# Loading the first input tile as one transfer instead of two halves on two queues

## The chip, the cores and the metric

The kernel runs on one core of a Trainium2 chip. Its time is the device time of one execution in microseconds (us), given as the median of several runs. A profile is one further execution, recorded by the hardware; its span runs from the first to the last instruction. The engines are TensorE (PE; its weight loads are listed apart as PEld), VectorE (DVE), ScalarE (ACT), GpSimd (POOL) and SyncE (SP). In this kernel SP and ACT issue DMAs, each into a queue of its own (q1 in the profile is SP's, q10 is ACT's), and both queues are served by the same 16 DMA engines.

## The reference

One mixer block and one MLP on an input of 2048 rows and 512 columns, in bfloat16:

```
h  = gelu(layernorm(x) @ w1)              # 512 x 512
hs = the four column quarters of h, shifted along the rows by +1, -1, +2, -2 (zeros come in)
x1 = x + hs @ w2                          # 512 x 512
out = x1 + gelu(layernorm(x1) @ w3) @ w4  # 512 x 1792, 1792 x 512
```

## The kernel before

The 2048 rows are 16 tiles of 128 rows; tile t holds, on partition p, row 16 p + t, so that each partition's row of a tile is 1 KB of contiguous memory. All weights and all of x stay in on-chip memory.

Each tile goes through the same steps. `stats` (L314, VectorE) and `aggr` (L317) give mean and variance. The inverse root comes, for tiles 0 to 3, from a square root on ScalarE (`rstd_act`, L325) and a reciprocal on VectorE (`rcp`, L331), and for later tiles from GpSimd (`rstd_pool`, L338 and L347). `norm` (L367 on VectorE) writes the normalized tile, which is transposed either by TensorE (`peT`, L389), with a copy out by ScalarE or VectorE (`evacT`, L401, L403), for tiles 0 to 9, or by a transposing DMA on SP (`dmaT`, L377) for the others. Then `mm1` (L440, and L456 for the first pair) multiplies two tiles at a time with w1, `gelu1` applies the activation, `mm2` (L515) multiplies with w2 and `add1` (L527) adds x. The second normalization, `mm3` (L542), `gelu2` (L555), `mm4` (L568) and the last addition (L582) follow, and `add2` stores each output tile (L586). The last output tile is done in two parts: 384 columns stored from SP's queue and then 128 columns stored from ACT's queue.

The order on each engine is written out by hand: a list of calls appends operations to one sequence per engine, and the `emit` function puts a semaphore wait ahead of an operation for each result that it needs and that its engine does not already know of. Every DMA has a semaphore of its own.

On VectorE the sequence starts: stats of tiles 0 and 1, their aggregates, stats of tile 2, reciprocal and norms of tiles 0 and 1, stats of tile 3, aggregates of 2 and 3, the copy of tile 1's transpose, reciprocal and norms of 2 and 3, stats of tiles 4 and 5, aggregates, stats of 6 and 7, norms of 4 and 5. TensorE begins with 12 multiplications of constants (`keep_warm`, L600), then the transposes of tiles 0 and 1, the first half of `mm1` of that pair, the transposes of tiles 2 and 3, the second half, three quarters of `mm1` of the second pair, and the transposes of tiles 4 and 5.

SP's queue issues all loads, one behind the other and without a wait: half of tile 0, tiles 1, 2 and 3 singly, w1 in two parts, tiles 4 and 5, 6 and 7, 8 to 11, 12 to 15, w2, w3. ACT's queue holds two DMAs in the whole kernel: the other half of tile 0 as ACT's first instruction, ahead of the load of the square root table (L590), and the last store.

Of the kernel before, what the change touches and what calls it, by code (L numbers as in the profile page):

```python
# [5 lines left out]
P = 128  # L6
# [151 lines left out]
def bass_standalone__mixer_s_mlp__prompt_kernel(  # L158
# [22 lines left out]
    x3 = x[0].rearrange("(p t) d -> p t d", t=NT)  # L181
# [3 lines left out]
    with ExitStack() as es:  # L185
        sb = lambda name, shape, dt: es.enter_context(nc.sbuf_tensor(name, shape, dt))
        x_sb = sb("x_sb", [P, NT, D], BF16)
# [25 lines left out]
        pr = Prog()  # L213
# [4 lines left out]
        g_x = [Gen() for _ in range(NT)]  # L218
# [18 lines left out]
        def load_x(eng, t0, n):  # L237
            pr.op(eng, f"x{t0}",
                  lambda e: e.dma_start(x_sb[:, t0 : t0 + n, :], x3[:, t0 : t0 + n, :]),
                  w=g_x[t0 : t0 + n], dma=True)  # L240

        def load_x_rows(eng, t, p0, n):
            pr.op(eng, f"x{t}_{p0}",
                  lambda e: e.dma_start(x_sb[p0 : p0 + n, t, :], x3[p0 : p0 + n, t, :]),
                  w=[g_x[t]], dma=True)

        def load_w(name, dst, src, c0=0, n=DC):

# [354 lines left out]
            pr.op("pe", "warm", f, w=[g])  # L603


        load_x_rows("sp", 0, 0, P // 2)
        load_x_rows("act", 0, P // 2, P // 2)
        for t in range(1, 4):
            load_x("sp", t, 1)
        load_w("w1", w1_sb, w1, 0, 2)  # L610
        load_w("w1", w1_sb, w1, 2, 2)
# [199 lines left out]
```

## Time and profile before

| what | value |
|---|---|
| time, median of 3 runs | 140.81 us (140.53 to 141.4) |
| profiled execution | 140.27 us |
| its span | 138.0 us |
| granted TensorE clock | 1.000 |
| issue of SP's half of tile 0 | 0.72 us, 2.4 us to landing |
| issue of ACT's half of tile 0 | 0.73 us, 3.0 us to landing |
| issue of tile 1 | 1.36 us, 2.7 us to landing |
| issue of tiles 4 and 5 | 3.90 us, 4.9 us to landing |
| first stats instruction (L314) | starts at 3.85 us |

The profile is read in views. The busy totals say how long each engine worked; the chain that ended last follows the work back from the last instruction, at each step to what released it; the timeline lists instructions in order of time; the list of waits adds up what each engine waited for. Times in views count from the start of the span. A DMA lands in 16 parts, one for each DMA engine, and the trace records when each part signalled; the DMA has landed when the last has.

### The profile page before, as it was taken

What the parts mean: (1) busy time and instruction counts of PE and PEld (TensorE: products, weight loads), DVE (VectorE), ACT (ScalarE), POOL (GpSimd) and SP (SyncE); (2) the same over time, 40 slices, a digit from 0 to 9 for tenths busy, and PEclk for the clock granted to TensorE, in tenths of its full rate; (3) what the DMA queues carried; (4) which work ended last, traced back from release to release, by engine and by line L of the source; (5) the groups of instructions that cost most, each with busy time, mean ns of one, the idle gap of its engine ahead of it and who ended that gap; (6) DMA issues with size and microseconds to landing.
All of it is one profiled execution on the core that took longest, in us unless ns stands there. A gap on an engine that the chain in (4) does not pass through costs nothing.

```text
span 138.0 us, 1802 instructions
## 1 busy us (share of the span) xinstructions
PE 131.6 (95%) x694; PEld 66.9 (48%) x706; DVE 50.2 (36%) x116; ACT 56.3 (41%) x71; POOL 16.9 (12%) x58
## 2 busy tenths in 40 slices
PE   7678999999999999999999999999999999999993
PEld 3265876665444444444444444444444444444452
DVE  0899999998958400000223000022300002232222
ACT  4097862496596796554000455400045540000000
POOL 2005342463333300000000000000000000000000
DMA  2899935434445499200111100011110001111111
GB/s 81 270 320 306 405 104 114 78 72 85 70 85 112 104 231 295 95 5 0 38 38 38 38 0 5 0 38 38 38 38 0 5 0 38 38 38 38 38 68 46
DMA packets 19047, 11.90 MB, mean 86 GB/s; under 512 B 12640, under 2 KB 18016, under 8 KB 19040
## 3 DMA queue, kind: packets, MB, share of 16 engines
q1 hardware_dynamic: 18816, 11.70, 30.7%
q10 hardware_dynamic: 224, 0.10, 0.3%
q8 instruction: 5, 0.08, 0.3%
q14 instruction: 2, 0.02, 0.0%
HBM read 6.82 MB, written 2.10 MB: 65 GB/s over the span
## 4 chain that ended last, share of the span: by engine, by line
PE 84%; DVE 10%; DMA 2%; ACT 1%; issue 1%; DVEq 0%
PE ps L568 35%; PE ps L542 35%; PE ps L515 8%; DVE st L314 6%; PE ps L440 5%; DMA x_sb<-in_x_dram 2%; DVE xn L367 1%; DVE x_sb L527 1%; DVE mv L317 1%; PE ps L389 1%; ACT xT L401 1%; ACT sdv L325 0%; DVE o_sb L582 0%; DVE rstd L331 0%; DVEq L134 0%
## 5 line engine op out<-in xcount | busy, mean ns | idle before, releaser
L542 PE MATMUL ps<-x1T,w_sb 128*128 128x512 bf16 x219 | 48.9, 379 | 0.3
L568 PE MATMUL ps<-w_sb,h2T 128*128 128x512 bf16 (+2 forms) x234 | 48.7, 366 | 0.2
L555 ACT ACTIVATE h2T<-ps 128x1024 bf16<-128x1024 f32 x28 | 28.3, 1020 | 39.0 <-PE ps L542 38.9
L582 DVE TENSOR_TENSOR o_sb<-ps,x_sb 128x512 bf16<-128x512 f32 (+2 forms) x17 | 11.2, 660 | 78.5 <-PE ps L568 78.5
L568 PEld LDWEIGHTS ps<-w_sb,h2T 128*128 128x128 bf16 x238 | 22.8, 98 | 25.9
L542 PEld LDWEIGHTS ps<-x1T,w_sb 128*128 128x128 bf16 x224 | 21.9, 98 | 26.4
L314 DVE BATCH_NORM_STATS2 st<-x_sb 128x6 f32<-128x512 bf16 x32 | 20.4, 675 | 3.9 <-DMA x_sb<-in_x_dram 3.9
L515 PE MATMUL ps<-w_sb,hT 128*128 128x512 bf16 x61 | 14.8, 379 | 0.2
L440 PE MATMUL ps<-xT,w_sb 128*128 128x256 bf16 x112 | 13.9, 273 | 0.5 <-ACT xT L401 0.4
L362 ACT ACTIVATE xn<-x_sb,nmr,rstd 128x512 bf16<-128x512 bf16 x16 | 12.0, 808 | 4.5 <-POOL nmr L352 4.5
L440 PEld LDWEIGHTS ps<-xT,w_sb 128*128 128x128 bf16 x112 | 10.7, 98 | 3.3 <-ACT xT L401 1.1
L527 DVE TENSOR_TENSOR x_sb<-ps,x_sb 128x512 bf16<-128x512 f32 x16 | 10.7, 683 | 3.1 <-PE ps L515 3.1
L347 POOL TENSOR_TENSOR rstd<-vpe,neghalf 128x2 f32<-128x2 f32 x14 | 9.9, 707 | 0.5
L515 PEld LDWEIGHTS ps<-w_sb,hT 128*128 128x128 bf16 x64 | 6.3, 98 | 6.3
L501 ACT ACTIVATE hT<-ps 128x1024 bf16<-128x1024 f32 x6 | 6.2, 1026 | 4.3 <-PE ps L440 4.3
L338 POOL TENSOR_SCALAR vpe<-mv 128x2 f32<-128x2 f32 x14 | 3.1, 220 | 28.4 <-DVE mv L317 28.3
L401 ACT ACTIVATE xT<-ps 128x512 bf16<-128x512 bf16 x9 | 4.9, 593 | 3.3 <-PE ps L389 3.3
L367 DVE TENSOR_SCALAR xn<-x_sb,mv,rstd 128x512 bf16<-128x512 bf16 x16 | 5.9, 410 | 0.3
L600 PE MATMUL ps<-const-bfloat16-1.0 128*128 128x512 bf16 x12 | 4.4, 542 | 0.8 <-PEq L796 0.8
L389 PE MATMUL ps<-ident,xn 128*128 128x128 bf16 x40 | 3.3, 220 | 1.4 <-DVE xn L367 1.3
L317 DVE BATCH_NORM_AGGREGATE mv<-st 128x2 f32<-128x6 f32 x32 | 4.5, 170 | 0.0
L389 PEld LDWEIGHTS ps<-ident,xn 128*128 128x128 bf16 x40 | 2.5, 98 | 2.5 <-DVE xn L367 2.2
(21 smaller groups left out, 16.5 us busy)
## 6 DMA issues: line engine op xcount, KB each, us to landing
w_sb<-in_w_dram SPq DMA_DIRECT2D x4, 512.0 KB, 4.7
out_dram<-o_sb SPq DMA_DIRECT2D x15, 128.0 KB, 1.8
w_sb<-in_w_dram SPq DMA_DIRECT2D x1, 1792.0 KB, 13.2
x_sb<-in_x_dram SPq DMA_DIRECT2D x2, 512.0 KB, 7.0
w_sb<-in_w_dram SPq DMA_DIRECT2D x3, 256.0 KB, 4.7
x_sb<-in_x_dram SPq DMA_DIRECT2D x2, 256.0 KB, 5.2
x_sb<-in_x_dram SPq DMA_DIRECT2D x3, 128.0 KB, 2.7
x1T<-xn SPq DMA_TRANSPOSE x16, 2.5
```

Of the source, the lines that this page charges most:

```text
L314: pr.op("dve", f"st{q}", lambda e: e.bn_stats(st6[:, q, :], a), r=[g], w=[g_st[q]])
L347: lambda e: e.tensor_tensor(rstd[:, q : q + 2], vpe[:, q : q + 2], neghalf[:], ALU.pow),
L362: lambda e: e.activation(xn[:, s, :], a, ACT_F.Identity, bias=nmr[:, q : q + 1], scale=rstd[:, q : q + 1]),
L367: lambda e: e.tensor_scalar(xn[:, s, :], a, mv[:, q, 0:1], rstd[:, q : q + 1], ALU.subtract, ALU.mult),
L389: ins = e.transpose(dst[:, P * c : P * (c + 1)], xn[:, q % NXN, P * c : P * (c + 1)], ident[:])
L440: ins = e.matmul(dst, w1_sb[:, dc, P * fc : P * (fc + 1)], xT[:, dc, 256 * p : 256 * (p + 1)], start=(dc == 0), stop=(dc == DC - 1))
L515: ins = e.matmul(bankap(b), hT[:, j, c : c + P], w2_sb[:, j, :], start=(j == 0), stop=(j == DC - 1))
L527: lambda e: e.tensor_tensor(x1_sb[:, t, :], bankap(b), x_sb[:, t, :], ALU.add),
L542: ins = e.matmul(bankap(b + i), w3_sb[:, dc, P * fc : P * (fc + 1)], x1T[:, dc, 512 * s : 512 * (s + 1)], start=(dc == 0), stop=(dc == DC ...
L555: pr.op("act", f"g2_{s}_{fp}", lambda e: e.activation(o, a, ACT_F.Gelu_apprx_tanh), r=gens, w=[g])
L568: ins = e.matmul(ps[:, 512 * b : 512 * b + n], h2T[:, fc, s % 2, P * i : P * (i + 1)], w4_sb[:, fc, c0 : c0 + n], start=(fc == 0), stop=(f ...
L582: lambda e: e.tensor_tensor(o_sb[:, s, 0:n], ps[:, 512 * b : 512 * b + n], x1_sb[:, t, c0 : c0 + n], ALU.add),
```

## The change

Tile 0 is loaded by one DMA of 128 rows on SP's queue, by the same helper and in the same loop as tiles 1 to 3. The DMA that ACT issued is gone, and with it the helper for loading some rows of a tile. All else is as it was; the lines below the helper have numbers that are 5 lower, and those below the loop 7 lower.

```diff
-        def load_x_rows(eng, t, p0, n):
-            pr.op(eng, f"x{t}_{p0}",
-                  lambda e: e.dma_start(x_sb[p0 : p0 + n, t, :], x3[p0 : p0 + n, t, :]),
-                  w=[g_x[t]], dma=True)
-
...
-        load_x_rows("sp", 0, 0, P // 2)
-        load_x_rows("act", 0, P // 2, P // 2)
-        for t in range(1, 4):
+        for t in range(4):
             load_x("sp", t, 1)
```

## The prediction

> **What bounds the kernel now.** I read the busy totals first, then the chain that ended last in order of time, then the timelines of VectorE and of the two queues. The totals:
>
> ```profile
> span 138.0 us, 1802 instructions
> PE 131.6 (95%) x694; PEld 66.9 (48%) x706; DVE 50.2 (36%) x116; ACT 56.3 (41%) x71; POOL 16.9 (12%) x58
> ```
>
> TensorE is busy for 95% of the span, so a change to one input load can only matter where TensorE isn't yet, or no longer, the bound. The chain (start, length, what) says where:
>
> ```profile
> 0.73 3.02 DMA x_sb<-in_x_dram
> ...
> 3.85 1.29 DVE st L314 x2
> ...
> 8.15 0.74 DVE xn L367 x2
> 8.89 1.25 DVE st L314 x2
> ...
> 11.56 0.42 DVE xn L367
> 11.98 0.05 issue
> 12.03 0.41 PE ps L389 x4
> ...
> 135.71 0.02 issue
> 135.73 0.29 DVE o_sb L582
> ```
>
> Up to 12.03 us the chain is the load of x tile 0 and then VectorE nearly without a gap; from 13.60 on it is TensorE back to back up to 135.71; then the last eviction, its store from ACT's queue and the end. A time saved or lost at 12.03 passes through to the end, because TensorE has no idle stretch later in which to absorb it (idle time after 12.03 is 1.05 us in total, in pieces). The change touches two places of this chain: its first row, and, through ACT's queue, its end.
>
> **The load of tile 0.** Issues of the two queues (start, length):
>
> ```profile
> 0.72 0.57 SPq L244 DMA_DIRECT2D x_sb<-in_x_dram  x1
> 0.73 0.57 ACTq L244 DMA_DIRECT2D x_sb<-in_x_dram  x1
> 1.36 0.56 SPq L239 DMA_DIRECT2D x_sb<-in_x_dram  x1
> ```
>
> From issue to landing these take 2.4, 3.0 and 2.7 us. The landing records put the last part of SP's half at 3.10, of ACT's half at 3.75 and of tile 1 at 4.08; st0 starts at 3.85, 0.10 after ACT's half. So ACT's half is the late one: its packets begin at 2.39 against 2.12 for SP's, and on four of the 16 engines its last rows come at 3.14 and later, after packets of tile 1.
>
> The changed kernel issues 128 rows at 0.72 on SP. The issue doesn't grow with the rows (0.57 for 64, 0.56 for the 128 of tile 1), so SP's later issues stay where they are; no instruction of theirs is moved past another. The trace has no 128-row load that comes first on an idle queue, so I bound its landing: from below SP's half, 2.38 us (3.10), since twice the rows can't land sooner; from above tile 3, issued at 2.43 and landed 3.9 us later into a backlog (0.72 + 3.9 = 4.64). The nearest row is tile 1, same shape and next in line: 2.72, so 3.45. I expect 3.3 to 3.45, 0.3 to 0.45 us before now.
>
> The Trainium skill (DMA: Bandwidth & Descriptors, section "Rules for kernel authors") says of two transfers to disjoint partition halves that they share the same engines either way, and advises one transfer of 128 partitions. The trace shows the shared engines (packets of both queues between 2.39 and 2.84), but also that the second half lands 0.65 us after the first. By the rule alone the front would change by 0 and the time stay at 140.8; by the rows tile 0 gains 0.3 to 0.45, and what becomes of that is the next step.
>
> **Who is late next.** Tile 1, then tile 3, then tiles 4 and 5. st1 needs tile 1 (4.08, and 0.1 for the wait: 4.18 against 4.46 now), st3 needs tile 3 (last part at 6.35, against its start at 6.68). So st3 can come forward by at most 0.33, and everything up to the second pair of norms by some 0.25 to 0.3. Then comes st4, which reads tiles 4 and 5:
>
> ```profile
> 6.36 0.41 DVE L367 TENSOR_SCALAR xn<-x_sb,mv,rstd 128x512 bf16<-128x512 bf16 x1
> 6.68 0.69 DVE L314 BATCH_NORM_STATS2 st<-x_sb 128x6 f32<-128x512 bf16 x1
> ```
>
> ```profile
> 8.48 0.41 DVE L367 TENSOR_SCALAR xn<-x_sb,mv,rstd 128x512 bf16<-128x512 bf16 x1
> 8.85 0.69 DVE L314 BATCH_NORM_STATS2 st<-x_sb 128x6 f32<-128x512 bf16 x1
> ```
>
> Where nothing is waited for, a stats instruction begins before the record of the norm ahead of it ends: 6.36 + 0.41 = 6.77 against 6.68, an overlap of 0.09. At st4 the overlap is 8.89 − 8.85 = 0.04: it started 0.045 us late. Tiles 4 and 5, issued at 3.90, land 4.9 us later; the last of their 16 parts is recorded at 8.82, the other 15 by 8.38. So st4 already waited for that load, too briefly for the list of waits to show. Whatever VectorE gains before it is turned into a wait there, unless the load comes earlier too.
>
> Does it? From 3.2 us on the DMA engines carry a backlog (busy share 0.88 in 3.2 to 4, 0.89, 0.71, 1.00, 0.81, 0.98 in the next stretches), so tiles 4 and 5 land when the slowest engine has moved its share of all bytes before them, and these bytes are the same: 512 KB of tiles 0 to 3, 512 KB of w1, 256 KB of tiles 4 and 5. Only one small completion packet of 9 ns per engine goes. In the front I therefore count **0.0**; bounds −0.36 (0.31 through tile 3's landing plus the 0.045) and, if the slowest part of tiles 4 and 5 shifts the other way by its lead over the rest (8.82 − 8.38), +0.44.
>
> **What goes from ACT.** Its DMA issue at 0.73 (0.57 us) goes, and with it the table load moves from 1.33 to about 0.73. Hidden: ACT then waits 2.6 us for VectorE's aggregates before its first sqrt, so nothing follows. One of two semaphore waits ahead of st0 (0.02) goes too, into the same wait at st4.
>
> **The end.** The last store, 32 KB, leaves by ACT's queue:
>
> ```profile
> 0.73 0.57 ACTq L244 DMA_DIRECT2D x_sb<-in_x_dram  x1
> ...
> 136.05 0.36 ACTq L586 DMA_DIRECT2D out_dram<-o_sb  x1
> ```
>
> It lands at 137.53, last of all (SP's last one at 137.2), so it is on the path. It is ACT's second DMA now and becomes its first. The trace prices a first DMA of this queue only at the start: 0.57 for the issue, against 0.36 for the second, and 1.66 us from issue to first packet, against 0.86. SP's first two take 0.57 and 0.56, later stores 0.33 to 0.36. Bounds: 0, if the start alone was slow (SP's second was as slow as its first, which speaks for that), and 0.86 → 1.66, **+0.8**, if all of it belongs to a queue's first use (part of that is a load's way through memory, so it is an outer bound). I take the difference of ACT's own two issues, **+0.2**.
>
> **Sum.** 0.0 + 0.2 = +0.2 us. The profiled execution took 140.27 (span 138.0 and 2.27 around it), so 140.5 by its own time. It lies 0.54 under the median of 140.81 and below the lowest of the three runs (140.53), so on the scale of the median: **141.0**. One per cent, 1.4 us, is about what a measurement of this kernel can tell from no change; this sum is far inside.
>
> **Rivals.**
> *The lead survives (faster).* Tiles 4 and 5 land earlier by 0.3, since one slow engine sets them and it may get its first rows sooner; then norms, transposes and TensorE all come forward by 0.25 to 0.3, and the end costs nothing: 140.81 − 0.3 = 140.5. For it: ACT's half is plainly the late piece of the first wait. Against it: 15 of 16 parts are there by 8.38 in any case, and the bytes ahead of the sixteenth are unchanged.
> *A straggler in tile 0 (slower).* With 128 rows in one ring per engine, the last part of tile 0 comes as late after its issue as that of tile 3: 4.64 against 3.75. st0 would start 0.89 later, st4 0.85 later (the 0.045 absorbs the rest), TensorE's transposes at 12.88 instead of 12.03: 140.81 + 0.85 = 141.7. It decides from the point at which tile 0 lands after 3.80. For it: two parts of tile 3 came over a microsecond behind the rest (6.18 and 6.35, the others by 5.16). Against it: nothing is ahead of tile 0 on any engine, while tile 3 had the 384 KB of tiles 0 to 2 before it.
> *The change does nothing where it counts.* The lead ends at st4 and ACT's first store costs no more than its second: 140.8.
>
> **How the numbers follow.** Forecast (lead lost at st4, first use of ACT's queue 0.2) 0.55; lead survives 0.17; straggler 0.13; nothing 0.15. The range reaches down to the faster rival's 140.5 less the 0.28 by which a run lies under the median, 140.2, and up to the straggler's 141.7 or the outer bound of the end (140.81 + 0.8 = 141.6), with a little scatter: 141.8. Slower by over 1% needs the straggler and the dear end together (142.5): 0.05. Faster by over 1% has no row behind it: 0.02. The rest, 0.93, lies within 1%.
>
> **What would show it.** Right: tile 0 lands at 3.3 to 3.45 and st0 starts 0.1 after it; st1 to the fourth norm 0.2 to 0.3 earlier; a wait of st4 for x of about 0.2 to 0.3 in the list of waits; transposes of tile 4 at 12.0 again; ACT's store issue at the end near 0.57. Wrong: tile 0 landing after 3.8, tiles 4 and 5 landing well away from 8.8 either way, or a last store that takes over 1.7 us to land.

## The result, and the profile after

| | before | after |
|---|---|---|
| time, median of 22 runs | 141.06 us | 140.45 us |
| ratio after / before | | 0.9951, 95% interval 0.9931 to 0.9972 |
| profiled execution | 140.27 us | 139.71 us |
| its span | 138.0 us | 137.4 us |

The change makes the kernel faster by half a per cent, 0.7 us, clear of the interval. The ratio and its interval leave out executions in the slower of two states that the chip has, two of the 22 after the change. The forecast was +0.2 us: the time lies inside its range, but the sign was wrong. TensorE's busy time did not fall (131.6 before, 132.1 after), so the span lost its 0.6 us elsewhere. Busy totals of the kernel after:

```profile
span 137.4 us, 1800 instructions
PE 132.1 (96%) x694; PEld 67.1 (49%) x706; DVE 50.2 (37%) x116; ACT 56.3 (41%) x71; POOL 16.9 (12%) x58
```

The chain that ended last, first 14 us, of the kernel after (start, length, what):

```profile
0.72 2.57 DMA x_sb<-in_x_dram
...
3.31 1.29 DVE st L309 x2
...
7.62 0.74 DVE xn L362 x2
8.35 1.19 DVE st L309 x2
...
9.76 1.18 DVE st L309 x2
...
10.98 0.73 DVE xn L362 x2
```

Tile 0 lands at 3.29 instead of 3.75, and the norms of tiles 4 and 5 start at 10.98 instead of 11.56: the 0.54 us that VectorE starts earlier, and the 0.045 us of the wait at st4 (stN is the stats instruction of tile N), reach TensorE whole. Of the 0.54 us, 0.46 are the landing; the other 0.08 come from st0, which starts 0.02 after its one load here and 0.10 after the later of its two before. This profiled execution, 139.71, is the second fastest of the 22 after the change, so what it shows is not yet the usual case. Two issues on SP's queue show a difference that the prediction had excluded (timeline of the kernel after):

```profile
0.72 0.40 SPq L239 DMA_DIRECT2D x_sb<-in_x_dram  x1
...
1.18 0.41 SPq L239 DMA_DIRECT2D x_sb<-in_x_dram  x1
...
3.57 1.89 SPq L239 DMA_DIRECT2D x_sb<-in_x_dram  x4
```

The last of these lines in the kernel before:

```profile
3.90 1.89 SPq L239 DMA_DIRECT2D x_sb<-in_x_dram  x4
```

The first two take 0.40 and 0.41 us, where the half of 64 rows and tile 1 behind it took 0.57 and 0.56. The first packet moves at 1.75 instead of 2.12, and every later load of SP is issued 0.33 us earlier (tiles 4 and 5 at 3.57, before at 3.90). And st4 does not wait (timeline of VectorE in the kernel after):

```profile
7.95 0.41 DVE L362 TENSOR_SCALAR xn<-x_sb,mv,rstd 128x512 bf16<-128x512 bf16 x1
8.27 0.69 DVE L309 BATCH_NORM_STATS2 st<-x_sb 128x6 f32<-128x512 bf16 x1
```

The overlap is 8.36 − 8.27 = 0.09 again, that of an instruction with nothing to wait for. Tiles 4 and 5 landed 4.1 us after their issue, at 7.66, 1.16 earlier than in the profile before. So the wait that was to swallow the lead was not there in this execution. The end costs next to nothing (timeline of ACT's queue in the kernel after):

```profile
135.47 0.38 ACTq L581 DMA_DIRECT2D out_dram<-o_sb  x1
```

ACT's only DMA takes 0.38 us to issue (0.36 before) and 0.88 us to its first packet (0.86 before).

### The profile page after: what moved, and what is told of

It is laid out like the page before. It is cut to its first block, busy times and chain, and to the rows that moved or that the text cites. A ratio compares the mean times of both kernels' runs of the same rounds, so it can differ in the third digit from the quotient of the medians.

```text
span 137.4 us, 1800 instructions
## 1 busy us (share of the span) xinstructions
PE 132.1 (96%) x694; PEld 67.1 (49%) x706; DVE 50.2 (37%) x116; ACT 56.3 (41%) x71; POOL 16.9 (12%) x58
## 4 chain that ended last, share of the span: by engine, by line
PE 78%; DVE 16%; DMA 4%; issue 1%; ACT 0%
PE ps L563 35%; PE ps L537 35%; DVE st L309 9%; PE ps L510 7%; DVE xn L362 3%; DMA x_sb<-in_x_dram 2%; DMA xT<-xn 2%; DVE mv L312 1%; DVE x_sb L522 1%; PE ps L435 1%; ACT sdv L320 0%; DVE o_sb L577 0%; DVE rstd L326 0%
## 5 line engine op out<-in xcount | busy, mean ns | idle before, releaser
L595 PE MATMUL ps<-const-bfloat16-1.0 128*128 128x512 bf16 x12 | 4.9, 594 | 0.8 <-PEq L789 0.8
L595 PEld LDWEIGHTS ps<-const-bfloat16-1.0 128*128 128x128 bf16 x12 | 1.7, 144 | 3.5 <-issue 3.5
```

Of the source, the lines that this page charges most:

```text
L595: ins = e.matmul(bankap(b), ones[:, 0:P], ones, start=True, stop=True)
```

## The experiments

Each kernel was timed in 5 rounds beside the kernel before, those with no interval given once. Kernels of one group below shared a chip, so ratios are compared within a group first; the changed kernel itself was timed in all groups but the first. A "second ring" in the expectations is the use of a second queue. The open questions were why SP's first issues were slow, whether tiles 4 and 5 come late in the kernel before by chance, and what moves their landing.

### First group: the slow issue, and the kernel before again

`halves_on_sp` (against the kernel before):

```diff
         load_x_rows("sp", 0, 0, P // 2)
-        load_x_rows("act", 0, P // 2, P // 2)
+        load_x_rows("sp", 0, P // 2, P // 2)
```

> Tile 0 is still two halves of 64 rows, but SP's queue issues both; ACT issues nothing at the start. Theory A (two queues issuing at the same time slow each other): SP's issues take about 0.40 us each, the first packet comes near 1.75, tile 0 lands at about 3.3 to 3.5, SP's later loads stand about 0.45 later than in the changed kernel and about 0.1 later than before; st4 starts near 8.3 to 8.5; time 0.3 to 0.6% under before. Theory B (a DMA of 64 rows is slow to issue): SP's first issues take 0.57 again, first packet near 2.1, time as before or slower.

Ratio 1.0003 (0.9967 to 1.004). Timeline of SP's queue:

```profile
0.73 0.56 SPq L244 DMA_DIRECT2D x_sb<-in_x_dram  x1
...
1.35 0.57 SPq L244 DMA_DIRECT2D x_sb<-in_x_dram  x1
...
1.97 0.58 SPq L239 DMA_DIRECT2D x_sb<-in_x_dram  x1
...
2.60 0.42 SPq L239 DMA_DIRECT2D x_sb<-in_x_dram  x1
```

With ACT silent, the two 64-row issues and the 128-row issue behind them are slow all the same. Theory A, two queues slowing each other, isn't needed for them; theory B, a DMA of 64 rows slow to issue and the one behind it too, fits. The first packet came at 2.06.

`act_spare_64` and `act_spare_late` (against the changed kernel; for the second the operation stands behind `act_table(ACT_F.Sqrt)`). Both move 64 KB more, into a buffer that nothing reads:

```diff
+        spare = sb("spare", [P, D], BF16)
...
+        pr.op("act", "spare", lambda e: e.dma_start(spare[0 : P // 2, :], x3[P - P // 2 : P, 0, :]),
+              w=[Gen()], dma=True)
         for t in range(4):
             load_x("sp", t, 1)
```

> The changed kernel, and ACT issues at the start a transfer of 64 rows of tile 0 into a buffer that nobody reads, so 64 KB more are moved. Theory A: SP's first two issues go back to about 0.57 and 0.56, its first packet to about 2.1, tile 0 lands near 3.6 to 3.8, and the time goes back to that of the kernel before (ratio 0.998 to 1.003). Theory B: SP's issues stay at 0.40, the first packet at 1.75, and the time stays 0.4 to 0.5% under before.

> The changed kernel, and the same spare transfer of 64 rows from ACT, but behind ACT's table load and first activation, so at about 2.2 us. The first three SP issues are undisturbed (0.40 each) and tile 0 lands at about 3.3 in both theories. Theory A: SP's issues that overlap it (tile 3 at 2.1, w1 at 2.6) take about 0.56 instead of 0.43 and all later loads stand 0.15 to 0.3 later; st4 still starts near 8.3, because tiles 4 and 5 land by 7.6; ratio about 0.995. If two queues slow each other only at the very start, SP's issues stay at 0.43.

Ratios 0.9973 (0.9941 to 1.0005) and 0.9993 (0.9957 to 1.0028). SP's issues of tiles 0 to 3 stayed at 0.40 to 0.43 in both, while ACT's own 64-row issue took 0.55 (timelines of the two queues in `act_spare_64`):

```profile
0.72 0.40 SPq L240 DMA_DIRECT2D x_sb<-in_x_dram  x1
...
0.73 0.55 ACTq L602 DMA_DIRECT2D spare<-in_x_dram  x1
```

Again the form, not the company: theory A falls. How much of the gain is left isn't told by the first ratio, whose interval holds 1 and 0.9951 alike, with no changed kernel on this chip beside it. In its profile tile 0 landed at 3.02, and yet tiles 4 and 5 landed at 9.79 and st4 started at 9.81. The late one went out at 1.54, earlier than expected, and its tiles 4 and 5 landed at 10.22.

`before_again` is the kernel before without an edit.

> The kernel before, profiled once more, for what varies between executions. If the slow issues belong to the kernel: 0.57, 0.57 and 0.56 again, first packet near 2.1. If the late landing of tiles 4 and 5 (8.82) was one execution's straggler: they land anywhere from 7.3 to 8.8 and st4 starts at 8.80 to 8.85, since VectorE is not ready before 8.80; if it belongs to the kernel, again 8.6 to 9.0.

Its issues were 0.57, 0.57 and 0.56 again. One time, 140.84. Timeline of VectorE:

```profile
7.71 0.74 DVE L367 TENSOR_SCALAR xn<-x_sb,mv,rstd 128x512 bf16<-128x512 bf16 x2
9.40 1.29 DVE L314 BATCH_NORM_STATS2 st<-x_sb 128x6 f32<-128x512 bf16 x2 [0.96 <-DMA x_sb<-in_x_dram]
```

Here tile 0 landed at 3.31, 0.44 us sooner than in the first profile, VectorE was ready for st4 at about 8.4, and st4 waited 0.96 us for tiles 4 and 5 (landed at 9.38). The span is 138.6, longer than the 138.0 of the first profile although tile 0 came sooner. These tiles landed 0.56 us apart in two executions of one kernel (8.82 and 9.38, the second later than either case of the expectation), and their landing, not tile 0, set this one.

### Second group: the late load taken out of the way

`after_again` is the changed kernel; `after_x4_early` and `before_x4_early` reorder SP's loads in the changed kernel and in the kernel before:

```diff
         load_w("w1", w1_sb, w1, 0, 2)
+        load_x("sp", 4, 2)
         load_w("w1", w1_sb, w1, 2, 2)
-        load_x("sp", 4, 2)
```

> The changed kernel once more, beside the next three on one chip. SP's first two issues again 0.40 and 0.41, first packet near 1.75, tile 0 at 3.0 to 3.3. Theory 1 (tiles 4 and 5 land now before, now after VectorE is ready at 8.27, whatever the kernel): they land anywhere from 7.5 to 10, and st4 waits in this execution if it is past 8.2; ratio 0.995 again. Theory 2 (the changed kernel makes them land early): 7.4 to 7.9.

> The changed kernel with the load of tiles 4 and 5 issued between the two parts of w1 instead of behind them. If the wait of st4 for this load takes part of the lead in many executions: it lands about 0.7 earlier, st4 starts at 8.0 to 8.3 without a wait, and the time falls below the changed kernel's by 0.2 to 0.5 us (ratio to before 0.990 to 0.993). If that wait is seldom or without weight: ratio as the changed kernel's, 0.995. If the second part of w1 becomes late instead (needed at 8.78, expected near 7.7): 0.997 or more.

> The kernel before with the same reordering of loads: tile 0 in two halves, tiles 4 and 5 between the parts of w1. It shows what the late load costs the kernel before, without the change. If the time of before is set by tiles 4 and 5: st4 starts at 8.4 to 8.85 without a wait, ratio 0.993 to 0.997, and the difference to the changed kernel with the same order is what tile 0 alone brings (0.1 to 0.54 us). If tile 0 alone sets it: ratio 0.999 to 1.001.

Ratios 0.9904 (0.987 to 0.9938), 0.994 (0.9903 to 0.9978) and 0.9952 (0.9927 to 0.9977). The reordering alone gives the kernel before about as much as the change did in the first comparison: its time did hang on that load. But it brings the changed kernel nothing (0.994 against 0.9904, where 0.990 to 0.993 was expected if st4's wait mattered). In the profiles the next load takes the place. Timeline of VectorE in `after_again`:

```profile
7.85 1.28 DVE L309 BATCH_NORM_STATS2 st<-x_sb 128x6 f32<-128x512 bf16 x2
9.05 0.30 DVE L312 BATCH_NORM_AGGREGATE mv<-st 128x2 f32<-128x6 f32 x2
10.34 1.29 DVE L309 BATCH_NORM_STATS2 st<-x_sb 128x6 f32<-128x512 bf16 x2 [0.99 <-DMA x_sb<-in_x_dram]
```

The same view of `after_x4_early`:

```profile
7.86 1.28 DVE L309 BATCH_NORM_STATS2 st<-x_sb 128x6 f32<-128x512 bf16 x2
9.05 0.30 DVE L312 BATCH_NORM_AGGREGATE mv<-st 128x2 f32<-128x6 f32 x2
10.89 1.29 DVE L309 BATCH_NORM_STATS2 st<-x_sb 128x6 f32<-128x512 bf16 x2 [1.54 <-DMA x_sb<-in_x_dram]
```

In both st4 runs without a wait and st6, which reads tiles 6 and 7, waits 0.99 and 1.54 us. In these two executions, what one late load lets through, the next one holds. With the reordering in both, the change is worth 0.0012 (0.994 against 0.9952), which the intervals can't tell from nothing.

`columns_two_queues` (shown against the kernel before) splits tile 0 by columns, so that both DMAs have 128 rows, of 512 B:

```diff
-        load_x_rows("sp", 0, 0, P // 2)
-        load_x_rows("act", 0, P // 2, P // 2)
+        load_x_cols("sp", 0, 0, D // 2)       # x_sb[:, t, c0 : c0 + n] <- x3[:, t, c0 : c0 + n]
+        load_x_cols("act", 0, D // 2, D // 2)
```

> The kernel before with tile 0 split by columns instead of rows: two DMAs of 128 rows and 256 columns (512 B rows) from SP and ACT. Theory B (64 rows are slow to issue, and the next issue with them): SP's issues take 0.40 and 0.41, first packet near 1.75, SP's later loads stand as in the changed kernel; tile 0 lands at 2.9 to 3.4, ratio 0.994 to 0.997. If a split over two queues costs by itself, through the second ring: SP's issues are fast and the ratio is still 0.998 to 1.001.

Ratio 0.9977 (0.9949 to 1.0005), against 0.9904 of the changed kernel beside it. Both issues took 0.40, tile 0 landed at 3.09, SP's later loads were issued as in the changed kernel, and most of the gain was missing. The changed kernel's 0.9904 rests on few executions, though (eight); against the 0.9951 of the first comparison, about half the gain is missing.

### Third group: one form of issue after another, and other splits

`issue_forms` (against the changed kernel) adds twelve loads that nothing reads, behind SP's last weight load:

```diff
+        for i, (p0, n) in enumerate([(0, 128), (0, 128), (0, 64), (0, 128), (0, 128), (64, 64),
+                                     (0, 64), (0, 128), (0, 128), (0, 32), (0, 128), (0, 128)]):
+            pr.op("sp", f"spare{i}",
+                  lambda e, i=i, p0=p0, n=n: e.dma_start(spare[p0 : p0 + n, i, :],
+                                                         x3[p0 : p0 + n, i, :]),
+                  w=[Gen()], dma=True)
```

> The changed kernel with twelve spare loads from SP behind its last weight load (near 53 us, when the DMA queue is otherwise empty), rows: 128, 128, 64, 128, 128, upper 64, lower 64, 128, 128, 32, 128, 128, into a buffer that nobody reads. Theory B: the issues of 64 and 32 rows take about 0.55 us and the issue behind each as well, those of 128 rows behind a 128-row one 0.40 to 0.43. If the slowness belongs to the start of a queue alone: all take 0.40 to 0.43.

Timeline of SP's queue, the second to the tenth of the twelve without the ninth:

```profile
53.15 0.43 SPq L764 DMA_DIRECT2D spare<-in_x_dram  x1
...
53.62 0.57 SPq L764 DMA_DIRECT2D spare<-in_x_dram  x1
...
54.23 0.57 SPq L764 DMA_DIRECT2D spare<-in_x_dram  x1
...
54.85 0.43 SPq L764 DMA_DIRECT2D spare<-in_x_dram  x1
...
55.33 0.47 SPq L764 DMA_DIRECT2D spare<-in_x_dram  x1
...
55.84 0.60 SPq L764 DMA_DIRECT2D spare<-in_x_dram  x1
...
56.48 0.58 SPq L764 DMA_DIRECT2D spare<-in_x_dram  x1
...
57.58 0.43 SPq L764 DMA_DIRECT2D spare<-in_x_dram  x1
```

In order: 128 rows 0.43, lower 64 rows 0.57, the 128 behind it 0.57, 128 again 0.43, upper 64 rows 0.47, lower 64 rows 0.60, the 128 behind it 0.58, and 32 rows 0.43. (The first, behind a weight load, took 0.47; the ninth, eleventh and twelfth, all of 128 rows, 0.42 to 0.43.) Far from the start of the queue, theory B holds for 64 rows and for the issue behind them; 32 rows are not slow, against the expectation, and the upper half is slow only a little in this place (as ACT's first DMA in the kernel before, and as SP's second in `halves_on_sp`, it took 0.57). A price per row is excluded. Why 64 rows cost more isn't known.

`tile1_on_act` and `columns_on_sp`, beside the changed kernel (`after_third`):

```diff
# tile1_on_act, against the changed kernel
-            load_x("sp", t, 1)
+            load_x("act" if t == 1 else "sp", t, 1)
# columns_on_sp, against columns_two_queues
-        load_x_cols("act", 0, D // 2, D // 2)
+        load_x_cols("sp", 0, D // 2, D // 2)
```

> The changed kernel a third time, beside the next two on one chip. Theory (span = start of st6 + 127.7 us, where st6 starts at the latest of VectorE's own readiness, the landing of tiles 4 and 5 plus 1.4, and the landing of tiles 6 and 7): the sum holds again within 0.15 us, whatever the landings are; ratio 0.990 to 0.995.

> The changed kernel, but tile 1 (128 rows) is issued by ACT, so that no 64-row transfer is left, both queues are used at the start, and SP's later loads are issued 0.46 us earlier than in the changed kernel. Theory R (traffic of a second ring delays the later loads by itself): tiles 4 to 7 land no earlier than in the changed kernel and the ratio is 0.996 to 1.000. Theory B alone (only the slow 64-row issue cost): tiles 4 to 7 land 0.3 to 0.46 earlier than in the changed kernel, ratio 0.988 to 0.992, below the changed kernel's. In both span = start of st6 + 127.7.

> Tile 0 as two transfers of 128 rows and 256 columns, both from SP: no second ring, no 64-row form, but SP's later loads 0.46 us later than in the changed kernel, 0.13 later than before. Theory R: the second ring was most of the cost, so ratio 0.993 to 0.996. Issue delay alone: tiles 4 to 7 land 0.1 later than before on the average, ratio 0.999 to 1.001.

Ratios 0.9947 (0.9917 to 0.9977), 0.9969 (0.994 to 0.9998) and 0.9979 (0.995 to 1.0009). `tile1_on_act` issues the later loads 0.48 us earlier than the changed kernel and still isn't faster; tile 0, which shared its start with tile 1 on the other queue, landed at 3.75 instead of 2.90. That speaks for a cost of the second queue (theory R), though the late tile 0 may be a part of it. `columns_on_sp` lies between the two expectations and doesn't decide between them. But it has the rows of 512 B without a second queue, issues the later loads 0.47 us later, and is 0.0032 above the changed kernel, less than 0.46 us of delay alone cost in the fourth group: so it gives no sign that rows of 512 B cost time by themselves.

### Fourth group: time of issue against a second queue

`later_loads_1` and `later_loads_2` put one or two spare loads of 16 KB between tile 3 and w1 in the changed kernel; `after_fourth` is the changed kernel and `columns_two_queues_2` the split by columns once more.

```diff
         for t in range(4):
             load_x("sp", t, 1)
+        for i in range(1):       # 2 in later_loads_2
+            pr.op("sp", f"spare{i}",
+                  lambda e, i=i: e.dma_start(spare[0:32, i, 0:256], x3[0:32, i, 0:256]),
+                  w=[Gen()], dma=True)
```

> The changed kernel beside the next three on one chip: ratio 0.990 to 0.996, SP's issues from 0.40, span = start of st6 + 127.7.

> The changed kernel with one spare load (32 rows of 512 B, 16 KB, read by nobody) on SP between tile 3 and w1, so that tiles 0 to 3 are issued as in the changed kernel and everything behind them 0.46 us later, that is 0.13 later than before. If the time of issue of the later loads carries the gain: tiles 4 to 7 land 0.3 to 0.46 later on the average and the ratio goes up by 0.002 to 0.0035, to 0.996 to 0.999. If the DMA engines' backlog sets the landing and the time of issue doesn't count: ratio as after_fourth within 0.001.

> The same with two spare loads: 0.93 us later. Time of issue counts: ratio up by 0.005 to 0.007 from the changed kernel's, to 0.998 to 1.002. Backlog alone: up by less than 0.002.

> Tile 0 as two halves of 256 columns from SP and ACT once more, now beside the changed kernel and the two with later loads. All of SP's issues stand as in the changed kernel, so if only the time of issue counts the ratio is that of after_fourth within 0.001; if a second ring at the start costs by itself, it is 0.003 to 0.007 above it, as on the other chip (0.9977 against 0.9904).

| kernel | later loads issued | second queue | ratio | interval |
|---|---|---|---|---|
| `after_fourth` | as after | no | 0.9902 | 0.9864 to 0.9940 |
| `later_loads_1` | +0.46 us | no | 0.9944 | 0.9912 to 0.9976 |
| `later_loads_2` | +0.92 us | no | 0.9989 | 0.9956 to 1.0021 |
| `columns_two_queues_2` | as after | yes | 0.9964 | 0.9930 to 0.9998 |

Time of issue counts: 0.0042 and 0.0087 of ratio, that is 0.6 and 1.2 us, for 0.46 and 0.92 us of delay. The first step lies within the intervals, the second is clear of them. The backlog alone, my reason for counting the front at nothing, would by the expectation have given less than 0.002. (The spare loads also move 16 and 32 KB; at the 200 to 350 GB/s that the DMA engines moved between 4 and 7 us in the kernel before, that is an estimated 0.05 to 0.16 us of the cost.) The second queue counts too: +0.0062 here, where the intervals overlap by 0.001, and +0.0073 on the other chip, where they don't, with SP's issues unmoved.

All groups together point the same way. With no second queue at the start the ratio rises with the delay of the later loads: 0.9902 to 0.9951 in four comparisons of the changed kernel, 0.9944 and 0.9979 at 0.46 and 0.47 us later (`later_loads_1`, `columns_on_sp`), 0.9989 and 1.0003 at 0.92 and 0.95 us later (`later_loads_2`, and `halves_on_sp`, whose tile 0 also lands late, at 3.65). With a second queue and SP's issues unmoved it is 0.9964 to 0.9993 (both splits by columns, both spare transfers). The sizes are less sure: the changed kernel had 0.9902 and 0.9904 from five and eight executions, and 0.9951 and 0.9947 from 22 and 12, and against the latter two the split by columns costs 0.0013 to 0.0030, 0.2 to 0.4 us. Timeline of VectorE in `columns_two_queues_2`, in which st4 and st6 both wait:

```profile
9.07 1.29 DVE L314 BATCH_NORM_STATS2 st<-x_sb 128x6 f32<-128x512 bf16 x2 [0.76 <-DMA x_sb<-in_x_dram]
10.27 0.30 DVE L317 BATCH_NORM_AGGREGATE mv<-st 128x2 f32<-128x6 f32 x2
11.04 1.29 DVE L314 BATCH_NORM_STATS2 st<-x_sb 128x6 f32<-128x512 bf16 x2 [0.47 <-DMA x_sb<-in_x_dram]
```

### What all profiles have in common

| kernel | st0 | st4 | st6 | span | span − st6 | last wait on a load |
|---|---|---|---|---|---|---|
| before | 3.85 | 8.85 | 10.27 | 137.99 | 127.7 | tiles 4, 5 (0.045 us) |
| before_again | 3.41 | 9.40 | 10.82 | 138.55 | 127.7 | tiles 4, 5 |
| after | 3.31 | 8.27 | 9.68 | 137.43 | 127.7 | tile 0 |
| after_again | 2.90 | 7.85 | 10.34 | 137.98 | 127.6 | tiles 6, 7 |
| after_third | 2.92 | 9.98 | 11.40 | 139.26 | 127.9 | tiles 4, 5 |
| after_fourth | 3.00 | 8.56 | 9.98 | 137.73 | 127.7 | tiles 4, 5 |
| halves_on_sp | 3.75 | 9.35 | 10.77 | 138.52 | 127.8 | tiles 4, 5 |
| act_spare_64 | 3.05 | 9.81 | 11.23 | 138.97 | 127.7 | tiles 4, 5 |
| after_x4_early | 2.91 | 7.86 | 10.89 | 138.53 | 127.6 | tiles 6, 7 |
| before_x4_early | 3.40 | 8.35 | 10.26 | 137.88 | 127.6 | tiles 6, 7 |
| columns_two_queues | 3.19 | 9.57 | 10.99 | 138.72 | 127.7 | tiles 4, 5 |
| columns_two_queues_2 | 3.16 | 9.07 | 11.04 | 138.81 | 127.8 | tiles 6, 7 |
| columns_on_sp | 3.15 | 9.47 | 10.89 | 138.63 | 127.7 | tiles 4, 5 |
| later_loads_1 | 3.09 | 8.09 | 9.51 | 137.27 | 127.8 | tiles 4, 5 (0.05 us) |
| later_loads_2 | 2.99 | 9.35 | 10.77 | 138.56 | 127.8 | tiles 4, 5 |
| issue_forms | 2.90 | 8.56 | 9.98 | 137.75 | 127.8 | tiles 4, 5 |

(Starts in us. The two profiles with a granted clock of 0.988, `act_spare_late` and `tile1_on_act`, have another sum and are left out.) In all sixteen the span is the start of st6 plus 127.6 to 127.9 us. So in these executions everything behind st6 has one length within 0.3 us, and the time is decided by which is latest: VectorE's way from tile 0 (4.95 us from st0 to st4 where nothing waits), the landing of tiles 4 and 5, or that of tiles 6 and 7. In 15 of the 16 it was one of the last two, in two of these by 0.05 us only.

## Why the prediction was wrong

*"The issue doesn't grow with the rows ..., so SP's later issues stay where they are": wrong, and the step that failed first.* I compared 0.57 us of a 64-row issue with 0.56 of a 128-row issue and concluded that rows are free. The 128-row issue was slow only because it stood behind a 64-row one; the other 128-row issues in the same trace took 0.41 to 0.47, and I had those rows. Removing the halves moved every later load by 0.33 us. The prediction's own sign of being wrong, tiles 4 and 5 landing well away from 8.8, is there in the profile after: 7.66.

*"In the front I therefore count 0.0", since the bytes ahead of tiles 4 and 5 are the same: wrong.* `later_loads_1` and `later_loads_2` show that time of issue passes through to the end, at about 1.3 us per us; an estimate from this for 0.33 us is 0.4 us. In the pair of profiles the front was worth 0.58 us. The DMA engines were busy, but a start 0.33 earlier may be a backlog that is through earlier; that this is the way in which it acts was not shown, and 1.3 us per us is more than it would give. And one profile's slowest part (8.82) isn't a property of the kernel: it came between 7.66 and 9.95 in four profiles of the changed kernel.

*"Whatever VectorE gains before it is turned into a wait there, unless the load comes earlier too": right, as a mechanism.* It did come earlier. The 0.045 us of missing overlap was a true sign: in `before_again` the same wait lasted 0.96 us. What I missed is the load behind it, tiles 6 and 7.

*"One of two semaphore waits ahead of st0 (0.02)": undersized.* In all seven profiles in which tile 0 comes as two transfers st0 starts 0.10 after the later one has landed, in all eleven with one transfer 0.02 after it: 0.08 us.

*Tile 0 lands at 3.3 to 3.45: 3.29 in the profile after, 2.88 to 2.98 in three further profiles of the same kernel.* Its nearest row, tile 1 at 2.72 us, carried the slow issue with it; without it, it is 2.15 to 2.57. The lower bound, SP's half at 2.38 "since twice the rows can't land sooner", carried it too, and three of the four profiles lie under it.

*The end, +0.2: oversized.* ACT's first DMA costs 0.02 us more to issue and 0.02 us more to the first packet. The 0.57 of ACT's issue at the start was the form of 64 rows, not a queue's first use: with 128 rows ACT's first issue took 0.40 in both splits by columns. `act_spare_64`, with an ACT DMA at the start, has 0.35 at the end, against 0.37 in `after_again`: the same 0.02.

*The rivals.* "The lead survives" gave 140.5, and 140.45 was measured, but that the figures meet is luck: the rival took 0.3 us off 140.81, the change took 0.7 off 141.06. Tiles 4 and 5 did land earlier, by 1.16 us in that pair of profiles; the reason given there, first rows that come sooner on one slow engine, was not tested. The straggler in tile 0 didn't occur: its last part never came after 3.30 in the changed kernel. The Trainium skill's advice (DMA: Bandwidth & Descriptors, section "Rules for kernel authors") to use one transfer rather than two partition halves agrees with what was measured, 0.9951; how the halves cost time, by the issue and through the second queue, is seen in these runs alone.

*What stays open.* How the gain divides between the earlier issue (about 0.4 us by the delays) and the absent second queue (0.9 to 1.0 us by the split into columns within its groups, 0.2 to 0.4 against the better measured ratios, with rows half as long) isn't settled; with the higher figures they make 1.3 to 1.4 us, the upper end of the 0.7 to 1.4 that the four comparisons of the changed kernel gave. Nor does their sum hold everywhere: with tiles 4 and 5 loaded earlier in both kernels, the change was worth 0.0012, less than 0.2 us, and no run says why. Why a second queue whose transfer has landed by 3.1 us (in the split by columns) should delay loads that land at 8 to 10 us was not shown.

## What to carry to other kernels

When several loads in a row feed a start-up chain, find the latest of them in more than one execution before pricing any: the one that gates can change from run to run, and the next one is often close behind it. Compare an issue's length with all issues of its kind, also with those that stand behind another form, because an issue can slow the next one. A busy DMA system doesn't make the time of issue free: here 0.92 us of later issue cost 1.2 us, though the DMA engines were busy for 0.58 or more of every microsecond from 3 to 10 us (`later_loads_2`).

## What the runs showed of the hardware that was not expected

A DMA of 64 rows takes 0.55 to 0.60 us to issue, from SP or ACT, at the start or at 53 us (in one place 0.47), and the 128-row issue behind it takes 0.56 to 0.58; 128 rows of one tile, first in a queue or behind another 128 rows of one tile, take 0.40 to 0.43 and 32 rows 0.43. Two queues issuing at the same moment don't slow each other (0.40 and 0.40 in `columns_two_queues_2`). The same load of 256 KB, issued at 3.57 to 3.58 us in four executions of one kernel, landed at 7.66, 7.77, 8.53 and 9.95 us. An instruction that waits for two loads started 0.10 us after the later had landed, with one load 0.02 us after it.
